# Block-sparse attention with a mixture of experts: the sparse scores of a tile's two query blocks in one stretch of TensorE's program

## The chip, the core and the metric

The kernel runs on one core of a Trainium2 chip. A core has engines that run side by side, each with an instruction queue of its own that it works off in order: TensorE (PE; PEld is its loading of weights), VectorE (DVE), ScalarE (ACT), GpSimd (POOL), and SyncE (SP), which issues most DMAs. Matmul results go to PSUM, which has eight banks of 128 partitions x 512 fp32 numbers. The engines wait for each other by semaphores. The metric is the device time of one execution in microseconds (us); lower is better.

## The reference

`q`, `k`, `v` are 4 batches x 8 heads x 768 tokens x 64. Tokens form 24 blocks of 32. A query block sees its own block and its two neighbours, the first and the last block, and three sampled blocks; the first and last query blocks see all keys. Each token's attention output (512 numbers over all heads) then goes to one of 8 experts.

```python
scores = scale * np.matmul(q, k.transpose(0, 1, 3, 2))
mask = np.abs(blk_i - blk_j) <= window
mask = mask | (blk_i == 0) | (blk_j == 0) | (blk_i == n_blocks - 1) | (blk_j == n_blocks - 1)
for qb in range(n_blocks):
    for kb in sampled_blocks[qb]:
        mask[qb * block:(qb + 1) * block, kb * block:(kb + 1) * block] = True
attn = np.exp(scores - max) / (sum + 1e-09)          # over the keys with mask
x = (attn @ v)                                       # 3072 tokens x 512
...
logits = x @ w_gate + modality_bias[modality_id]
e_idx = np.argmax(logits, axis=1)
out = gate_w * (np.maximum(x @ w1[e_idx], 0.0) @ w2[e_idx])
```

## The kernel before

**Two stages.** First attention for 24 tiles of 128 tokens (two of them are the "dense" blocks that see all keys), with the gate's logits and the ranking of tokens by expert beside it; then the experts, a matrix product in three fp32r parts per group of 256 tokens. The change is in the first stage.

**A sparse tile.** Batches come in halves of two (HB = 2). Per half there are NM = 11 sparse tiles; a tile is two neighbouring query blocks (n = 0 and 1) of both batches of the half, all 8 heads. That makes 22 tiles and, with n and the batch b, four items per tile, in the order (n, b) = (0,0), (0,1), (1,0), (1,1). A query block sees 8 key blocks. POOL copies the keys into `kbuf` (lines 466 to 482): slots 0 to 7 are the eight for n = 0 and slots 4 to 11 those for n = 1, so four are shared.

**Steps of an item** (letters as in the code) and their lines:
- S, `scores` (line 533): 16 matmuls, 64 rows x 32 columns of the array each, fp32, for both batches of one n, so it is done once per n, at the item with b = 0. It writes two fresh banks. An fp32 matmul is two passes, so a block of scores shows as 32 records.
- M, `masked` (541, DVE): adds the mask and takes the maximum; it reads and, with the last item, frees the scores' banks.
- X, `exps` (549, ACT); T, `transposed` (558, PE: four 128x128 transposes into a bank); A, `copied` (563, ACT: out of that bank).
- per tile: W, `weigh_shared` (580, PE) and V, `sum_rows` and `weigh_own` (573, 589, PE), O, `divide` (440 to 442, DVE: frees V's and W's banks), Y, `turned` (596 PE, 598 ACT), G, the gate (606 PE, 609 DVE), then small DVE work for the routing (295 to 368).

Dense items have the same letters: scores 379, maxima 392 to 395, exp 401 and 402, transposes 411, copies 418, weighing 431 and 433.

**What sets the order.** Each engine's program in this stage is written in the order of the code. A loop over ticks t does, for every step, the item k = t - LAG[step]; LAG says how many ticks behind its scores an item's step stands (M 1, X 2, T and A 4, W 5, V 7, O 8, Y 10, G 13 for sparse items). Within a tick the steps come in the order of ORDER. Items of the second half's dense blocks are put between sparse items 21|22, 29|30, 45|46 and 47|48 (DENSE_AFTER). Items 21, 29 and 45 have (n, b) = (0, 1), so in the sixth, eighth and twelfth tile two dense items stand between the n = 0 and the n = 1 items. The opening of the program, the first tile and part of the second, is a list written by hand (START).

**PSUM.** All eight banks come from one pool; `bank()` hands out a free one, and the first write into it waits until its last reader is done. A block of scores takes two banks, a transpose, a weighing, a gate one each; a pair of dense scores takes four.

Of the kernel before, what the change touches and what calls it, by code (L numbers as in the profile page):

```python
# [38 lines left out]
HB = 2  # L39
NM = NB // 2 - 1  # L40
# [49 lines left out]
def attention_moe(ctx, tc, kD, qD, qH, v0, v1, blocks, modality, w_gate, bias, w1, w2, out):  # L90
# [29 lines left out]
    with ExitStack() as actx:  # L120
# [5 lines left out]
        def bank():  # L126
            return psum.tile([P, 512], F32, name="bank")
# [244 lines left out]
        def dense_scores(b, pr):  # L372
            q = qd[b // HB]
            s1, s2 = zip(*[(bank(), bank()[:, 0:256]) for _ in range(2)])
            for o, blocks_ in ((s1, slice(0, 16)), (s2, slice(16, 24))):
                for c in range(2):
                    for u in range(2):
                        r, col = slice(64 * u, 64 * u + 64), 64 * (u ^ c)
                        nc.tensor.matmul(o[c][col:col + 64, :], lhsT=q[r, b % HB * NPAIR + pr + c], rhs=kd[b][r, pr // 2, blocks_, c * 32:c * 32 + 32],
                                         start=True, stop=True, tile_position=(64 * u, col))  # L380
            return zip(s1, s2)
# [8 lines left out]
        def dense_max(b, pr, s1, s2):  # L390
            nm2 = small.tile([P, 2], F32, name="nm2")
            nc.vector.tensor_reduce(nm2[:, 0:1], s1, axis=AX.X, op=ALU.max, negate=True)
            nc.vector.tensor_reduce(nm2[:, 1:2], s2, axis=AX.X, op=ALU.max, negate=True)
            nb_ = small.tile([P, 1], F32, name="nb_")
            nc.vector.tensor_scalar(nb_, nm2[:, 0:1], nm2[:, 1:2], 0.125, ALU.min, ALU.mult)
            return s1, s2, nb_

        def dense_exp(b, pr, s1, s2, nb_):
            a = work.tile([P, 768], F32, name="a", bufs=5)
            sm = small.tile([P, 2], F32, name="sm", bufs=6)  # L400
            nc.scalar.activation(a[:, 0:512], s1, AF.Exp, bias=nb_, scale=0.125, accum_out=sm[:, 0:1])  # L401
            nc.scalar.activation(a[:, 512:768], s2, AF.Exp, bias=nb_, scale=0.125, accum_out=sm[:, 1:2])
            return a, sm

        def dense_transpose(b, pr, a, sm):
            tps = []
            for k0, k1 in ((0, 4), (4, 6)):
                tp = bank()
                tps.append((k0, k1, tp))
                for k in range(k0, k1):  # L410
                    nc.tensor.transpose(tp[:, (k - k0) * P:(k - k0 + 1) * P], a[:, k * P:(k + 1) * P], ident)
            return tps, sm

        def dense_copy(b, pr, tps, sm):
            at = ad[0]
            ad.append(ad.pop(0))
            for k0, k1, tp in tps:
                (nc.vector.tensor_copy if (b, pr) in DENSE_DVE else nc.scalar.copy)(at[:, k0:k1, :].rearrange("p a b -> p (a b)"), tp[:, 0:(k1 - k0) * P])
            su = small.tile([P, 1], F32, name="su", bufs=4)
            nc.vector.tensor_tensor(su, sm[:, 0:1], sm[:, 1:2], ALU.add)  # L420
            return at, su


        def dense_weigh(b, pr, at, su):
            o = bank()
            for k in range(-1, 6):
                for u in range(2):
                    h, col = 2 * pr + u, 64 * (u ^ pr % 2)
                    r = slice(64 * u, 64 * u + 64)
                    if k < 0:  # L430
                        nc.tensor.matmul(o[r, D:D + 1], lhsT=ident[:, col:col + 64], rhs=su, start=True, stop=False, tile_position=(0, 64 * u))
                    else:
                        nc.tensor.matmul(o[r, 0:D], lhsT=at[:, k, col:col + 64], rhs=vd[b][:, k, D * h:D * h + D],
                                         start=False, stop=k == 5, tile_position=(0, 64 * u))
            return (o,)
# [89 lines left out]
        def scores(q, g, n):  # L525
            s0 = 4 * n
            kv = kbuf[g % 2].rearrange("p s (b r f) -> p s b r f", b=HB, r=NPAIR)
            sp = [bank(), bank()]
            for b in range(HB):
                for pr in range(NPAIR):  # L530
                    for u in range(2):
                        r = slice(64 * u, 64 * u + 64)
                        nc.tensor.matmul(sp[u][32 * pr:32 * pr + 32, b * 256:(b + 1) * 256], lhsT=q[r, b * NPAIR + pr, n, :],  # L533
                                         rhs=kv[r, s0:s0 + 8, b, pr, :], start=True, stop=True, tile_position=(64 * u, 32 * pr))
            return sp
# [682 lines left out]
        qraw, o_s = {}, {}  # L1218
# [39 lines left out]
        for g in range(2 * NM):  # L1258
            half, m = divmod(g, NM)
# [20 lines left out]
        st, done = {}, set()  # L1280

        def do(op, it):
            if (op, it) in done:
                return
            done.add((op, it))
            if it[0] == "d":
                _, b, pr = it
                half = b // HB
                if op == "S":
                    if pr % 2 == 0:  # L1290
                        for c, o in enumerate(dense_scores(b, pr)):
                            st["d", b, pr + c] = o
                elif op == "M":
                    st[it] = dense_max(b, pr, *st[it])
                elif op == "X":
                    st[it] = dense_exp(b, pr, *st[it])
                elif op == "T":
                    st[it] = dense_transpose(b, pr, *st[it])
                elif op == "A":
                    st[it] = dense_copy(b, pr, *st[it])  # L1300
                elif op == "W":
                    st[it] = dense_weigh(b, pr, *st[it])
                elif op == "O":
                    if (b % HB, pr) == (0, 0):
                        new_tile(-1, half)
                    dense_out(b, pr, *st.pop(it))
                elif (b % HB, pr) == (HB - 1, NPAIR - 1):
                    if op == "Y":
                        turns[-1, half] = turned(xrs[-1, half])
                    elif op == "G":  # L1310
                        end_tile(-1, half)
            else:
                _, half, m, n, b = it
                if op == "S":
                    if b == 0:
                        sp = scores(qraw[m, half], half * NM + m, n)
                        for b_ in range(HB):
                            st["s", half, m, n, b_] = sp
                elif op == "M":
                    st[it] = masked(m, n, b, st[it])  # L1320
                elif op == "X":
                    if (n, b) == (0, 0):
                        sums[m, half] = small.tile([P, 4, 2], F32, name="sums", bufs=4)
                    st[it] = exps(sums[m, half][:, 2 * b + n, :], *st[it])
                elif op == "T":
                    st[it] = transposed(n, st[it])
                elif op == "A":
                    if n == 0:
                        ats[m, half, b] = work.tile([P, 16, 2, 32], F32, name="at", bufs=NAT)
                    copied(n, b, st.pop(it), ats[m, half, b])  # L1330
                    if (n, b) == (1, HB - 1):
                        sums[m, half] = spread(sums[m, half])
                elif (n, b) == (1, HB - 1):
                    if op == "W":
                        st[it] = bank()
                        weigh_shared(half * NM + m, st[it], [ats[m, half, b_] for b_ in range(HB)])
                    elif op == "V":
                        banks[m, half] = bank()
                        sum_rows(sums.pop((m, half)), banks[m, half])
                        weigh_own(half * NM + m, st[it], [ats[m, half, b_] for b_ in range(HB)])  # L1340
                    elif op == "O":
                        new_tile(m, half)
                        divide(st.pop(it), banks.pop((m, half))[:, 0:H], slice(0, P), H, xrs[m, half][:, 0:HD])
                    elif op == "Y":
                        turns[m, half] = turned(xrs[m, half])
                    elif op == "G":
                        end_tile(m, half)
# [98 lines left out]
```

## Time and profile before

| | us |
|---|---|
| median of 3 runs | 539.94 |
| the runs | 538.39, 539.94, 546.9 |
| the profiled execution | 535.39 |
| its span, first to last instruction | 533.7 |
| score matmuls (line 533), first and last start | 23.5, 215.1 |

All times in the rows below are from that one profiled execution, in us from the span's start. A timeline row has the start, the length (from the first start to the last end of the instructions that the row merges), engine, line, operation, the tile written <- the tiles read, the shape, the count, and in brackets how long the engine had been idle before and what ended that. PE's instructions overlap: the next one starts long before the row's end. A row of a group has the busy time in total, the mean length of one instruction in ns, and the idle time before its instructions.

### The profile page before, as it was taken

The page shows a single profiled execution, that of the slowest core. Times are in us where ns is not written, and L with a number is a line of the kernel's source. Part 1 is how long each engine was busy: PE and PEld are TensorE (multiplying, and loading weights), DVE is VectorE, ACT ScalarE, POOL GpSimd, SP SyncE. Part 2 cuts the span into 40 slices and gives each one's busy share as a digit, 9 for nine tenths or more (in the row PEclk, how much of TensorE's full clock was granted, in tenths as well). Part 3 has the DMA queues.
Part 4 walks back from the last instruction along what each step waited for, and adds up shares of the span by engine and source line. Part 5 has one row for each costly group of instructions (what it writes and reads, how often), then busy time and mean ns, then how long its engine had stood idle before and what let it go on. Part 6 is the DMA issues. An engine that isn't in the chain of part 4 may idle for free.

```text
span 533.7 us, 19015 instructions
## 1 busy us (share of the span) xinstructions
PE 512.8 (96%) x7298; PEld 433.4 (81%) x7298; DVE 378.7 (71%) x1139; ACT 335.4 (63%) x765; POOL 214.7 (40%) x451
## 2 busy tenths in 40 slices
PE   8999999998999999899999999999999999999995
PEld 6667676776778777788989898998989899898984
DVE  7995588677778999967996655556565555656553
ACT  3689877977888977935456454646545464554552
POOL 3578675666458886123155123030312303031213
PEclk9999999999999999999999999999999999999999
DMA  7985886999646888965788776676757667675740
GB/s 281 339 243 150 234 252 209 249 223 242 205 144 205 209 217 233 277 206 206 237 280 305 237 253 201 239 252 204 239 191 244 211 222 250 206 243 192 249 150 23
DMA packets 49443, 119.44 MB, mean 224 GB/s; under 512 B 7744, under 2 KB 8128, under 8 KB 49344
## 3 DMA queue, kind: packets, MB, share of 16 engines
q1 hardware_dynamic: 45248, 105.02, 64.6%
q0 software_dynamic: 4096, 13.12, 6.9%
q8 instruction: 59, 0.97, 0.8%
q14 instruction: 40, 0.33, 0.2%
HBM read 105.52 MB, written 12.86 MB: 222 GB/s over the span
## 4 chain that ended last, share of the span: by engine, by line
issue 41%; PE 32%; DVE 11%; DMA 7%; POOL 5%; SPq 3%; ACT 1%; POOLq 0%; DVEq 0%; ACTq 0%
PE bank L533 5%; PE bank L558 5%; DMA out<-slot,si 3%; PE bank L589 3%; DVE y L541 3%; POOL slot L736 3%; DMA slot<-v 3%; PE bank L580 2%; POOL out L790 2%; PE bank L606 2%; PE bank L754 1%; PE bank L770 1%; PE bank L771 1%; PE bank L769 1%; PE bank L755 1%
## 5 line engine op out<-in xcount | busy, mean ns | idle before, releaser
L725 DVE TENSOR_TENSOR slot<-slot 128x1024 fp32r<-128x1024 f32 x99 | 122.8, 1245 | 89.5 <-ACT slot L722 87.7
L722 ACT CAST slot<-slot 128x1024 fp32r<-128x1024 f32 x104 | 108.1, 1048 | 104.1 <-PE bank L755 50.1
L754 PE MATMUL bank<-slot 128*128 128x256 f32 x384 | 108.4, 282 | 0.0
L756 PE MATMUL bank<-slot 128*128 128x256 f32 x384 | 107.7, 281 | 0.0
L755 PE MATMUL bank<-slot 128*128 128x256 f32 x384 | 107.6, 280 | 0.0
L790 POOL DMA_INDIRECT out<-slot,si x20 | 25.4, 1270 | 178.6 <-ACT slot L786 175.6
L549 ACT ACTIVATE a<-y,mn 128x256 f32<-128x256 f32 x176 | 88.6, 511 | 10.3 <-DVE mn L541 10.2
L769 PE MATMUL bank<-slot 128*128 128x512 f32 x192 | 76.6, 399 | 0.0
L770 PE MATMUL bank<-slot 128*128 128x512 f32 x192 | 75.9, 395 | 0.0
L771 PE MATMUL bank<-slot 128*128 128x512 f32 x192 | 75.7, 394 | 0.0
L754 PEld LDWEIGHTS bank<-slot 128*128 128x128 f32 x384 | 72.2, 188 | 0.6
L755 PEld LDWEIGHTS bank<-slot 128*128 128x128 f32 x384 | 72.1, 188 | 0.4
L756 PEld LDWEIGHTS bank<-slot 128*128 128x128 f32 x384 | 72.2, 188 | 0.0
L541 DVE CUSTOM_DVE_ANT_1 y<-bank,smask 128x256 f32<-128x256 f32 x176 | 66.3, 417 | 0.4
L482 POOL COPY slot<-slot 128x128 f32 x264 | 63.9, 295 | 0.0
L563 ACT COPY at<-bank 128x512 f32<-128x512 f32 x88 | 50.7, 577 | 9.9 <-PE bank L558 9.9
L504 POOL TENSOR_SCALAR slot<-slot 32x1024 f32<-32x1024 f32 x40 | 41.6, 1041 | 35.4 <-issue 11.6
L558 PE MATMUL bank<-ident,a 128*128 128x128 f32 x352 | 51.9, 280 | 0.8 <-ACT a L401 0.5
L533 PE MATMUL bank<-slot,q_raw 64*32 64x256 f32 x1408 | 49.4, 382 | 1.5 <-issue 0.6
L771 PEld LDWEIGHTS bank<-slot 128*128 128x128 f32 x192 | 36.1, 188 | 8.4
L770 PEld LDWEIGHTS bank<-slot 128*128 128x128 f32 x192 | 36.1, 188 | 7.8 <-DVE slot L725 0.4
L558 PEld LDWEIGHTS bank<-ident,a 128*128 128x128 f32 x352 | 38.1, 140 | 4.9 <-ACT a L549 0.8
(302 smaller groups left out, 852.9 us busy)
## 6 DMA issues: line engine op xcount, KB each, us to landing
slot<-w SPq DMA_DIRECT2D x100, 512.0 KB, 4.1
slot<-v SPq DMA_DIRECT2D x180, 128.0 KB, 3.9
x_d<-xr SPq DMA_DIRECT2D x22, 256.5 KB, 5.0
q_raw<-qH SPq DMA_DIRECT2D x22, 256.0 KB, 4.8
slot<-v SPq DMA_DIRECT2D x16, 256.0 KB, 4.6
slot<-kD SPq DMA_DIRECT2D x13, 256.0 KB, 4.3
slot<-v SPq DMA_DIRECT2D x4, 768.0 KB, 11.8
slot<-w SPq DMA_DIRECT2D x10, 256.0 KB, 4.1
```

The costliest lines, as they stand in the source:

```text
L533: nc.tensor.matmul(sp[u][32 * pr:32 * pr + 32, b * 256:(b + 1) * 256], lhsT=q[r, b * NPAIR + pr, n, :], rhs=kv[r, s0:s0 + 8, b, pr, :], st ...
L541: nc.vector.tensor_tensor_reduce(y[:, u, :].rearrange("p (s f) -> p s f", s=8), sp[u][:, b * 256:(b + 1) * 256].rearrange("p (s f) -> p s ...
L549: nc.scalar.activation(a[:, u, :], y[:, u, :], AF.Exp, bias=mn[:, u:u + 1], scale=-1.0, accum_out=total[:, u:u + 1])
L558: nc.tensor.transpose(tp[:, k:k + P], a[:, u, c * P:(c + 1) * P], ident)
L722: nc.scalar.copy(h, s)
L725: (eng or (nc.gpsimd if n in POOL_SPLITS else nc.vector)).tensor_tensor(l, s, h.bitcast(F32), ALU.subtract)
L754: nc.tensor.matmul(o, lhsT=h[:, fs], rhs=xh[g % 2][:, c, :], start=c == 0 and f % 2 == 0, stop=False)
L755: nc.tensor.matmul(o, lhsT=h[:, fs], rhs=xl[g % 2][:, c, :], start=False, stop=False)
L756: nc.tensor.matmul(o, lhsT=l[:, fs], rhs=xh[g % 2][:, c, :], start=False, stop=c == 3 and f % 2 == 1)
L769: nc.tensor.matmul(o, lhsT=hh[0][:, f, ts_], rhs=h[:, fs], start=f == 0, stop=False)
L770: nc.tensor.matmul(o, lhsT=hh[0][:, f, ts_], rhs=l[:, fs], start=False, stop=False)
L771: nc.tensor.matmul(o, lhsT=hl[f // 4][:, f % 4, ts_], rhs=h[:, fs], start=False, stop=f == 7)
```

## The change

The n = 1 block of scores of a tile is computed where its n = 0 block is, directly behind it, in all tiles but the first of the first half (whose scores stand in the hand-written opening). The four banks are taken at that place; everything else of the code stays.

```diff
                 if op == "S":
                     if b == 0:
-                        sp = scores(qraw[m, half], half * NM + m, n)
-                        for b_ in range(HB):
-                            st["s", half, m, n, b_] = sp
+                        for n_ in (n,) if (half, m) == (0, 0) else range(2) if n == 0 else ():
+                            sp = scores(qraw[m, half], half * NM + m, n_)
+                            for b_ in range(HB):
+                                st["s", half, m, n_, b_] = sp
```

Only PE's program changes its order; the same instructions stand on DVE, ACT, POOL and SP in the same order. On PE the number of instructions is the same too. Three places follow. L533 are the scores, L558 a tile's transposes, L573 and L589 step V, L580 step W, L596 step Y, L606 the gate; `x16` is one block of scores.

PE, an ordinary tile (its second block is the first row with a minus, the next tile's blocks follow):

```order
 L596 MATMUL bank<-ident,xr 128x128 x4
 L558 MATMUL bank<-ident,a 128x128 x4
-L533 MATMUL bank<-slot,q_raw 32x256 x16
 L573 MATMUL bank<-rexp,fold 32x8 x4
 L589 MATMUL bank<-slot,at 32x64 x32
 L558 MATMUL bank<-ident,a 128x128 x8
-L533 MATMUL bank<-slot,q_raw 32x256 x16
+L533 MATMUL bank<-slot,q_raw 32x256 x32
 L606 MATMUL bank<-wg_raw,xT 64x8 x8
 L580 MATMUL bank<-slot,at 64x64 x16
```

The second block has left its place between transposes and step V, and stands ahead of the gate and step W, five rows earlier in its own tile.

PE, the eighth tile, which has dense scores (L379) between its two blocks and the dense step O (L431, L433) behind the first; the program before:

```order
L533 MATMUL bank<-slot,q_raw 32x256 x16
L431 MATMUL bank<-su,ident 64x1 x2
L433 MATMUL bank<-slot 64x64 x12
L580 MATMUL bank<-slot,at 64x64 x16
L558 MATMUL bank<-ident,a 128x128 x8
L379 MATMUL bank<-slot,qd 64x512 x4
L379 MATMUL bank<-slot,qd 64x256 x4
L606 MATMUL bank<-wg_raw,xT 64x8 x8
L573 MATMUL bank<-rexp,fold 32x8 x4
L589 MATMUL bank<-slot,at 32x64 x32
L558 MATMUL bank<-ident,a 128x128 x8
L533 MATMUL bank<-slot,q_raw 32x256 x16
```

and the changed one:

```order
L533 MATMUL bank<-slot,q_raw 32x256 x32
L431 MATMUL bank<-su,ident 64x1 x2
L433 MATMUL bank<-slot 64x64 x12
L580 MATMUL bank<-slot,at 64x64 x16
L558 MATMUL bank<-ident,a 128x128 x8
L379 MATMUL bank<-slot,qd 64x512 x4
L379 MATMUL bank<-slot,qd 64x256 x4
L606 MATMUL bank<-wg_raw,xT 64x8 x8
L573 MATMUL bank<-rexp,fold 32x8 x4
L589 MATMUL bank<-slot,at 32x64 x32
L558 MATMUL bank<-ident,a 128x128 x8
L580 MATMUL bank<-slot,at 64x64 x16
```

The second block moved ahead of ten rows, the dense scores among them; behind the last transposes step W now follows at once.

PE, the last tile, with the semaphores that an instruction waits for (a name is the engine whose progress is awaited):

```order
 L533 MATMUL bank<-slot,q_raw 32x256 [waits DVE_49]
 L533 MATMUL bank<-slot,q_raw 32x256 x14
-L606 MATMUL bank<-wg_raw,xT 64x8 [waits DVE_49]
+L533 MATMUL bank<-slot,q_raw 32x256 [waits DVE_49,Pool_49]
+L533 MATMUL bank<-slot,q_raw 32x256 [waits DVE_49]
+L533 MATMUL bank<-slot,q_raw 32x256 x6
+L533 MATMUL bank<-slot,q_raw 32x256 [waits Pool_49]
+L533 MATMUL bank<-slot,q_raw 32x256 x7
+L606 MATMUL bank<-wg_raw,xT 64x8 [waits Activation_49]
 L606 MATMUL bank<-wg_raw,xT 64x8 x7
```

The second block's first two matmuls, one for each of its banks, wait for DVE, which by the program's counts has to finish lines 440 and 442 of step O first; the gate now takes a bank that ACT has to free.

## The prediction

> **What bounds the kernel now.** I read the page first: the span, the engines' shares and the slices of time.
>
> ```profile
> span 533.7 us, 19015 instructions
> PE 512.8 (96%) x7298; PEld 433.4 (81%) x7298; DVE 378.7 (71%) x1139; ACT 335.4 (63%) x765; POOL 214.7 (40%) x451
> PE   8999999998999999899999999999999999999995
> DVE  7995588677778999967996655556565555656553
> PEclk9999999999999999999999999999999999999999
> ```
>
> TensorE (PE) is busy nearly throughout and its clock is never throttled. The score matmuls (line 533) run in the first 40% of the span, and there VectorE (DVE) has slices of 9 too. So I asked for the engines' busy time by stage.
>
> ```profile
> 44.00:60.00 16.00, 14.86 (x415) 11.49 (x417) 10.04 (x50) 14.09 (x48) 11.96 (x33) 1.00 0.78 211
> 82.00:95.00 13.00, 12.13 (x291) 8.93 (x289) 10.78 (x49) 9.37 (x31) 6.42 (x19) 1.00 0.66 204
> 193.00:201.00 8.00, 7.70 (x220) 6.01 (x219) 7.68 (x38) 6.12 (x21) 6.81 (x20) 1.00 0.87 229
> 201.00:209.00 8.00, 7.97 (x214) 6.18 (x212) 7.81 (x41) 7.43 (x24) 4.75 (x11) 1.00 0.82 238
> 300.00:360.00 60.00, 60.00 (x399) 54.78 (x398) 35.63 (x38) 29.85 (x37) 14.01 (x12) 1.00 0.71 232
> ```
>
> The columns are the length, then busy time of PE, its weight loads, DVE, ACT, POOL, then clock and DMA. The mixture of experts (300 to 360) has PE busy for all of 60.00: whatever the attention stage gains or loses arrives at the end undiminished. In the attention stage it is not one engine: from 193 to 209 DVE is busy 7.68 and 7.81 of 8.00, as much as PE. A tile is a loop PE, DVE, ACT, PE, and a saving on PE counts only where that loop has slack.
>
> **What the change saves: changes of the array's shape.** An ordinary tile, PE's timeline (start, length, what):
>
> ```profile
> 47.09 0.60 PE L596 MATMUL bank<-ident,xr 128*128 128x128 f32 x4
> 47.52 0.60 PE L558 MATMUL bank<-ident,a 128*128 128x128 f32 x4
> 48.05 1.09 PE L533 MATMUL bank<-slot,q_raw 64*32 64x256 f32 x32
> 49.08 0.25 PE L573 MATMUL bank<-rexp,fold 128*32 128x8 f32 x8
> ```
>
> Four transposes followed by more transposes take 47.52 - 47.09 = 0.43 us; four followed by the scores take 48.05 - 47.52 = 0.53. Going into the 64x32 shape costs 0.10. The scores hold PE for 49.08 - 48.05 = 1.03. The 32 passes last 1.09 from the first start to the last end.
>
> ```profile
> L533 PE MATMUL bank<-slot,q_raw 64*32 64x256 f32 x1408 | 49.4, 382 | 1.5 <-issue 0.6 <-DVE xrd L452 0.5 <-DMA q_raw<-qH 0.4
> ```
>
> One pass is 0.382 long, so the starts spread over 1.09 - 0.38 = 0.71 us. Eight tile positions run side by side, so that is four rounds with three intervals, at most 0.24 each, about 0.22. A second block of 16 matmuls in the same stretch thus costs 4 x 0.22 = 0.87 instead of 1.03: 0.16 saved. The way in (0.10) is saved as well only where the neighbours left behind have one shape; here they are 128*128 (L558) and 128*32 (L573), so a change stays. I take 0.16 per tile; 21 tiles make 3.4 us, the most I give the change on this account (0.26 in each would be 5.5).
>
> The Trainium skill, page TensorEngine Tiling (Array Packing), section Key Properties, says that a change of tiling mode drains the array. If a drain meant waiting for the whole matmul in flight, removing one would save about that flight, 0.38 per tile, and the sum would be 8.0 us, an estimate from the rule. The rows do not bear that out: the way in costs 0.10 while a pass lasts 0.38, so most of the flight is overlapped.
>
> Added work: none. No instruction, DMA or byte is added, and DVE, ACT, POOL and SP keep their order; only PE's moves. The second block now needs POOL's gathered keys 0.87 us after the first one's start, some us earlier than before. The tightest tile is the one at 36.48:
>
> ```profile
> 32.77 2.91 POOL L482 COPY slot<-slot 128x128 f32 x11
> 36.48 1.10 PE L533 MATMUL bank<-slot,q_raw 64*32 64x256 f32 x32 [0.46 <-DVE xrd L452]
> ```
>
> The copies end at 35.68, the second block is due at 36.48 + 0.87 = 37.35: hidden by 1.7 us, cost nothing. Queries are one load for both blocks, so SP has no new deadline.
>
> **What it costs: 0.87 us in front of everything behind the first block, and two more banks held.** In PE's queue the second block now stands ahead of the gate (L606), the weighing (L580), the transposes and, in three tiles, the dense scores (L379); all of these come 0.87 later, and who waits for them waits longer. Where it used to stand nothing covers ACT's copies any more. The tile where this bites, PE, then DVE, then ACT:
>
> ```profile
> 82.21 1.09 PE L533 MATMUL bank<-slot,q_raw 64*32 64x256 f32 x32
> 87.61 0.64 PE L606 MATMUL bank<-wg_raw,xT 128*64 128x8 f32 x16
> 89.27 1.10 PE L558 MATMUL bank<-ident,a 128*128 128x128 f32 x8
> 90.30 1.09 PE L533 MATMUL bank<-slot,q_raw 64*32 64x256 f32 x32
> 93.09 0.66 PE L558 MATMUL bank<-ident,a 128*128 128x128 f32 x4 [0.54 <-ACT a L401]
> 95.05 0.44 PE L411 MATMUL bank<-ident,a 128*128 128x128 f32 x2 [0.36 <-ACT a L401]
> ```
>
> ```profile
> 88.30 0.17 DVE L609 TENSOR_TENSOR lg<-bank,btok 128x8 f32<-128x8 f32 x1 [1.25 <-PE bank L606]
> 89.43 0.69 DVE L442 TENSOR_TENSOR xr<-bank,rt 128x512 f32<-128x512 f32 x1 [0.46 <-PE bank L589]
> ```
>
> ```profile
> 82.11 0.58 ACT L598 COPY xT<-bank 128x512 f32<-128x512 f32 x1
> 90.73 0.57 ACT L563 COPY at<-bank 128x512 f32<-128x512 f32 x1
> 92.26 0.69 ACT L401 ACTIVATE a<-bank,nb__2462 128x512 f32<-128x512 f32 x1 [0.96 <-DVE nb__2462 L395]
> ```
>
> Read as a loop: DVE waits 1.25 us for PE's gate and 0.46 for L589, ACT waits 0.96 for DVE, PE waits 0.54 and 0.36 for ACT. Every link is bound, so 0.87 at 82.21 becomes 0.87 at 93.09. The 1.03 given back at 90.30 is worth nothing: behind the transposes (ending 89.27 + 1.10 = 90.37) PE would come to L580 at once, and the bank it needs is let go by ACT's copy ending 90.73 + 0.57 = 91.30; the scores had covered that. To this comes the wait for the second block's own banks: the copy at 82.11 ends at 82.69, due is 82.21 + 0.87 = 83.08, a slack of 0.39, less than the 0.87 that the tile before may hand on: up to 0.48 more, and once more the 0.87 that is handed on. Lower end 0.87, upper end 0.87 + 0.48 + 0.87 = 2.2. I take 2.0, near the upper end, because this loop has no idle link to work a lag off.
>
> Two more tiles have dense scores between their blocks, so that two of the eight banks are held 7.6 and 9.7 us:
>
> ```profile
> 59.96 1.09 PE L533 MATMUL bank<-slot,q_raw 64*32 64x256 f32 x32
> 67.56 1.26 PE L533 MATMUL bank<-slot,q_raw 64*32 64x256 f32 x32
> 119.80 1.09 PE L533 MATMUL bank<-slot,q_raw 64*32 64x256 f32 x32
> 123.57 0.97 PE L580 MATMUL bank<-slot,at 128*64 128x64 f32 x25 [1.83 <-issue]
> 129.50 1.09 PE L533 MATMUL bank<-slot,q_raw 64*32 64x256 f32 x32
> ```
>
> I price the first at 0.9 (the lower end: the tiles before it run with PE ahead), the second at 1.5 (between the ends: its 1.83 of idle time with no releaser could swallow part). The three together: 4.4, bounds 2.6 and 6.6.
>
> The late tiles, from 185 on, run at DVE's pace. The last one:
>
> ```profile
> 209.03 1.09 PE L533 MATMUL bank<-slot,q_raw 64*32 64x256 f32 x32
> 210.46 0.64 PE L606 MATMUL bank<-wg_raw,xT 128*64 128x8 f32 x16 [0.33 <-DVE rt L440]
> 211.52 1.15 PE L580 MATMUL bank<-slot,at 128*64 128x64 f32 x32 [0.43 <-issue]
> 214.15 1.36 PE L533 MATMUL bank<-slot,q_raw 64*32 64x256 f32 x32
> ```
>
> ```profile
> 210.73 0.69 DVE L442 TENSOR_TENSOR xr<-bank,rt 128x512 f32<-128x512 f32 x1
> ```
>
> Its second block, due at 209.90, has to wait for the bank that DVE reads until 211.42. It then ends the stretch near 211.42 + 0.87 + 0.16 = 212.45, and the gate comes 2.0 later than at 210.46; the 0.43 behind it is absorbed and the 1.03 of the old place is given back: + 0.6. The other three late tiles lie between -0.16 (DVE keeps up) and + 0.87 (bound like the tile at 82); I take the middle, 0.35, since DVE is neither idle nor all of the limit: + 1.05. Late tiles: + 1.6, bounds 0.1 and 3.2.
>
> **The sum.** 21 tiles are merged: 3 with dense scores between, 4 late ones, 14 ordinary. 14 x (-0.16) = -2.2; dense + 4.4; late + 1.6: together + 3.8 us. The profiled execution took 535.39 with a span of 533.7, and would become 539.2; the median of the runs is 539.94, 4.55 above it, and the sum on that is 543.7.
>
> **The rivals.**
> The other side: banks are always free in time and the loop absorbs 0.87. Then each tile gains 0.16 and the time is 539.94 - 3.4 = 536.5. For it: PE's waits for banks are hardly seen before (1.5 us idle in all ahead of L533). Against it: the bound loop at 82 to 95. It decides at the slack of DVE's gate and ACT's copies: above 0.87 in all three dense tiles it wins. Its far end is that each change of shape costs the whole flight of a pass, 0.38: 21 x 0.38 = 8.0 and 532; the 0.10 of the way in speaks against that. [...]
> Nothing to measure: the gain of the ordinary tiles and the dense tiles' loss cancel because waits at L401 reset PE's lead either way: 540.
> The loop is bound in every tile: 21 x 0.87 = 18.3 us more, 558. For it: 7.81 of 8.00 on DVE late. Against it: from 44 to 60 DVE is busy 10.04 of 16.00 and can catch up.
>
> **How the numbers follow.** My forecast, between + 0.5 and + 9 us: chance 0.60. Gain on all tiles: 0.18, of which 0.03 for the drain in full. Cancelled: 0.13. Bound in every tile: 0.09. Range: low 536.5, the first rival; high 549.0, which takes the upper bounds of the dense and late tiles, 6.6 + 3.2, with half of the ordinary gain lost: 6.6 + 3.2 - 1.1 = 8.7 and rounding. About 2% is what a measurement of this kernel can tell from no change, that is 529 and 551. Slower by over 2%: 0.09 and little else, 0.09; faster by over 2%: 0.03; within 2%: 0.88.
>
> **What would show it.** Right: the line of the scores gathers fewer switches, 23 stretches on PE instead of 44, each pair 1.9 us long; the waits of PE L533, L580 and L606 for ACT L563 and for DVE grow by several us; DVE's wait for L606 grows; attention ends some 4 us later. If the last scores' tile ends earlier and DVE's wait for L606 has not grown, the loop had slack and I am wrong. If PE's lag grows evenly over all tiles, the third rival is right. If the lag is only at 60 to 72, 82 to 95 and 120 to 131, the banks held across the dense scores are the cause.

## The result, and the profile after

The changed kernel takes 542.87 us (median of 6 runs, 541.92 to 544.55). Against the runs of before beside them its ratio is 1.0141, interval 1.0103 to 1.0178, so about 7.6 us (5.5 to 9.6) slower. Run once more on another occasion it took 543.29 us with a ratio of 1.0100 (1.0057 to 1.0143), 5.4 us. Both lie within 2%. All ratios compare fast executions alone: the 546.9 among before's three runs is not in them, nor are four of the experiments' executions that took 656 to 1247 us. The forecast was 543.7, 3.8 us more than before. The profiled execution took 543.24 us with a span of 541.5, that of before 533.7.

The page of the changed kernel, span, engines and two rows of the slices:

```profile
span 541.5 us, 19001 instructions
PE 516.4 (95%) x7298; PEld 440.6 (81%) x7298; DVE 374.9 (69%) x1139; ACT 335.0 (62%) x765; POOL 216.2 (40%) x451
PE   8999898997999999889999999999999999999995
PEclk9999999998999999999999999999999999999999
```

PE's share falls from 96% to 95% with the same 7298 records. Of the 7.8 us by which the span grew, 4.2 are idle time of PE and 3.6 are busy time, although no work was added; part of that is a stretch at half the clock, the one 8 that is new in the clock's row, of which more below. Two groups of PE's line view:

```profile
L533 PE MATMUL bank<-slot,q_raw 64*32 64x256 f32 x1408 | 47.5, 380 | 4.5 <-issue 2.7 <-DMA q_raw<-qH 0.5 <-DVE rt L440 0.4
L580 PE MATMUL bank<-slot,at 128*64 128x64 f32 x704 | 26.7, 228 | 4.1 <-issue 3.2 <-POOL slot L504 0.9
```

The scores are busy for 47.5 us instead of 49.4: the shared stretches save something. POOL is not among the three largest releasers of the scores: its keys are in time, but for one place named below. The view of the waits, first of before, then of the changed kernel (us in total, times, the longest):

```profile
ACT at L563 <- PE bank L558: 9.9, 13, 1.7
DVE lg L609 <- PE bank L606: 7.5, 10, 1.3
```

```profile
ACT at L563 <- PE bank L558: 19.6, 17, 4.8
DVE lg L609 <- PE bank L606: 15.9, 15, 2.8
```

DVE waits twice as long for the gate, ACT twice as long for the transposes: PE brings later what the others need. The place, in PE's timeline of the changed kernel, is the first tile with dense scores between its blocks (it starts at 59.96 in before):

```profile
57.21 1.96 PE L533 MATMUL bank<-slot,q_raw 64*32 64x256 f32 x64
59.09 0.64 PE L606 MATMUL bank<-wg_raw,xT 128*64 128x8 f32 x16
...
65.25 0.25 PE L573 MATMUL bank<-rexp,fold 128*32 128x8 f32 x8 [0.30 <-ACT at L563]
...
67.49 0.66 PE L558 MATMUL bank<-ident,a 128*128 128x128 f32 x4 [0.23 <-DVE xr L442]
...
69.58 1.15 PE L580 MATMUL bank<-slot,at 128*64 128x64 f32 x32 [0.87 <-POOL slot L504]
```

The stretch with both blocks takes 59.09 - 57.21 = 1.88 us. Behind the dense scores PE then waits three times: 0.30 and 0.23 for banks, and 0.87 ahead of step W, where the second block used to stand.

Where the 7.8 us of the span come from, from the starts of the same instructions in both traces: the tile at 59.96 +2.8, that at 82.21 +2.1, that at 119.80 +4.2, together +9.1; all other attention about -1.5; the experts +0.3. So the cost sits in the three tiles that the prediction named. The experiments ask whether that is the change or chance, and what in those tiles it is.

### The profile page after: what moved, and what is told of

It is laid out like the page before. It is cut to its first block, busy times and chain, and to the rows that moved or that the text cites. A ratio compares the mean times of both kernels' runs of the same rounds, so it can differ in the third digit from the quotient of the medians.

```text
span 541.5 us, 19001 instructions
## 1 busy us (share of the span) xinstructions
PE 516.4 (95%) x7298; PEld 440.6 (81%) x7298; DVE 374.9 (69%) x1139; ACT 335.0 (62%) x765; POOL 216.2 (40%) x451
## 4 chain that ended last, share of the span: by engine, by line
issue 41%; PE 29%; DVE 9%; DMA 8%; POOL 6%; ACT 3%; SPq 2%; POOLq 1%; ACTq 0%; DVEq 0%
PE bank L533 7%; PE bank L558 6%; PE bank L589 4%; PE bank L580 3%; DMA slot<-v 3%; POOL slot L736 3%; DMA out<-slot,si 2%; POOL out L790 2%; PE bank L606 2%; DMA slot<-x_d,gi 2%; PE bank L596 1%; PE bank L433 1%; DVE slot L725 1%; PE bank L411 1%; SPq L521 1%
## 5 line engine op out<-in xcount | busy, mean ns | idle before, releaser
L504 POOL TENSOR_SCALAR slot<-slot 32x1024 f32<-32x1024 f32 x40 | 42.5, 1062 | 56.4 <-PE bank L589 31.4
L482 POOL COPY slot<-slot 128x128 f32 x264 | 63.9, 293 | 0.0
L563 ACT COPY at<-bank 128x512 f32<-128x512 f32 x88 | 50.7, 576 | 19.6 <-PE bank L558 19.6
L558 PE MATMUL bank<-ident,a 128*128 128x128 f32 x352 | 53.2, 282 | 1.3 <-DVE xr L442 0.7
L533 PE MATMUL bank<-slot,q_raw 64*32 64x256 f32 x1408 | 47.5, 380 | 4.5 <-issue 2.7
L558 PEld LDWEIGHTS bank<-ident,a 128*128 128x128 f32 x352 | 38.3, 141 | 6.2 <-DVE xr L442 1.4
```

Source lines behind the costliest of these rows:

```text
L558: nc.tensor.transpose(tp[:, k:k + P], a[:, u, c * P:(c + 1) * P], ident)
```

## The experiments

The tiles are counted from 0 here; 5, 7 and 11 are the three with dense scores between their blocks, "crossing" below. us are the ratio times 538, the median of before.

**Only the crossing tiles, and all but them.** In place of the diff's condition:

```diff
-for n_ in (n,) if (half, m) == (0, 0) else range(2) if n == 0 else ():
+for n_ in (n,) if half * NM + m not in (5, 7, 11) else range(2) if n == 0 else ():
```

> Only the sixth, eighth and twelfth tile are merged, the three that have dense scores between their two blocks; the other 18 tiles stand as before. Theory T (the cost sits in these three): the trace of the changed kernel is 2.8, 2.1 and 4.2 us later behind them, 9.1 in all, so +9 us on 537.3, ratio 1.017 (1.012 to 1.020). Rival E (each merged tile costs the same): 7.6 us over 21 tiles is 0.36 each, three make +1.1, ratio 1.002. Rival I (PE's idle time with no releaser, which in the changed kernel is 2.74 at 125.03 and 1.62 at 225.07 against 1.83 and 0.31 before, makes most of the difference): +2.2 only, if both fall in the same places, ratio 1.004.

Measured: 1.0112 (1.0044 to 1.0180), +6.0 us from three tiles. The other way round, merging all but those (condition `in (0, 5, 7, 11)`):

> The other 18 tiles are merged, the three with dense scores between their blocks stand as before. Theory T: the rest of the changed kernel's lag, 7.8 - 9.1 = -1.3 us, ratio 0.998 (0.995 to 1.000). Rival E: 18 x 0.36 = +6.5 us, ratio 1.012. Rival I: +2.2 or what stalls there are, ratio 1.004.

Measured: 1.0004 (0.9968 to 1.0041), +0.2 us from eighteen tiles. An even cost, rival E, is out on both sides. Theory T stands, with less than the 9 that one pair of traces gave and just under the 1.012 at which its range began. Rival I's 1.004 lies just below the first interval and inside the second, so these two times alone do not put it out; the rows without such idle times, further down, do.

**The others, early and late.** Merged alone: tiles 1 to 4, 6 and 8 to 10; then tiles 12 to 21.

> Only the early tiles without dense scores between their blocks are merged: the second to fifth, the seventh, and the ninth to eleventh, eight of 22. By the terms of the prediction 8 x (-0.16) = -1.3 us, ratio 0.998. By the trace of the changed kernel (2.75 us earlier by the sixth tile, 1.6 more over the seventh, nothing over the ninth to eleventh) up to -4 us, ratio 0.992. Rival E: 8 x 0.36 = +2.9, ratio 1.005.

> Only the last ten tiles of 22 are merged, behind the last dense scores. By the terms of the prediction: six ordinary ones -1.0, four late ones +1.6, together +0.6 us, ratio 1.001 (0.998 to 1.004). Rival (the late loop on DVE is bound in each): 10 x 0.87 = +8.7, ratio 1.016. The trace of the changed kernel is 2.9 us later over this stretch, of which 1.3 at one idle time of PE without a releaser: ratio 1.003 to 1.005 if that falls there again.

Measured: early 0.9969 (0.9934 to 1.0003), -1.7 us; late 1.0025 (0.9989 to 1.0062), +1.3 us. The late loop bound in each tile (1.016) is out. The two signs are as forecast, but each interval reaches to no change.

**The banks alone.** Before's order, with the first two of the second block's sixteen matmuls, one for each of its banks, moved ahead in the crossing tiles:

```diff
-            sp = [bank(), bank()]
+            sp = st.pop(("held", g), None) or [bank(), bank()]; nx = [bank(), bank()] if n == 0 and g in (5, 7, 11) else None
-            for b in range(HB):
-                for pr in range(NPAIR):
-                    for u in range(2):
+            for b, n_, bk in ((0, n, sp), (1, n, sp), *(((0, 1, nx),) if nx else ())):
+                for pr in range(NPAIR) if bk is not nx else (0,):
+                    for u in range(2) if n == 0 or (b, pr) != (0, 0) or not g in (5, 7, 11) else ():
...
+                                         rhs=kv[r, 4 * n_:4 * n_ + 8, b, pr, :], start=True, stop=True, tile_position=(64 * u, 32 * pr))
-            return sp
+            return st.update({("held", g): nx} if nx else {}) or sp
```

> Before's order, but in the three tiles with dense scores between the blocks the first two of the second block's sixteen matmuls, one for each of its two banks, stand behind the first block; the other fourteen stay where they were. So the banks are held as in the change, while only about an eighth of 0.87 us of PE's work is moved ahead. Theory Ta (the cost is the two of eight banks held across the dense scores): most of the 9 us remains, +6 to +9 us, ratio 1.011 to 1.017. Theory Tb (the cost is 0.87 us of work put in front of a loop PE, DVE, ACT, PE that is bound): three times an eighth, +0.3 us, ratio 1.001 and at most 1.003. Half and half would show as 1.006 to 1.009.

Measured: 1.0088 (1.0044 to 1.0131), +4.7 us, in the band named for half and half; Theory Tb alone (at most 1.003) is out, the lower part of Ta's range is not. PE's timeline, the first and the third crossing tile:

```profile
59.75 1.49 PE L533 MATMUL bank<-slot,q_raw 64*32 64x256 f32 x36
61.17 0.41 PE L606 MATMUL bank<-wg_raw,xT 128*64 128x8 f32 x8
...
66.00 0.25 PE L573 MATMUL bank<-rexp,fold 128*32 128x8 f32 x8 [0.30 <-ACT at L563]
...
68.16 0.66 PE L558 MATMUL bank<-ident,a 128*128 128x128 f32 x4 [0.23 <-DVE xr L442]
...
121.35 2.03 PE L533 MATMUL bank<-slot,q_raw 64*32 64x256 f32 x36
```

The two bank waits, 0.30 and 0.23, are those of the full change, to the hundredth: they come from holding two banks, since the run with the work alone, next, has neither. In the third tile the 36 records last 2.03, in the first 1.49: there the matmuls into the held banks wait as well. One thing was wrong in the expectation: the two moved matmuls are not an eighth of 0.87. The 36 records hold PE for 61.17 - 59.75 = 1.42 us where a block of 32 holds it for 1.02, and the 28 left behind still take 1.01. So 0.4 us per tile, 1.2 of the 4.7, are work in front of the loop; by itself that would be a ratio of 1.002, below the interval.

**The work alone.** Before's order and banks, the first block computed twice in the crossing tiles:

```diff
-            for b in range(HB):
+            for b in (0, 1, 0, 1) if n == 0 and g in (5, 7, 11) else range(HB):
```

> Before's order and banks; in the three tiles with dense scores between the blocks the first block is computed twice in its stretch, into the same banks, so that 0.87 us of work is put in front of the loop, no bank is held longer, and the second block keeps its place. This adds 3 x 0.87 = 2.6 us of work to PE. Theory Tb (the loop is bound and the cost of the change is what is put in front of it): +2.6 us or more, each tile as much later as the change makes it (2.8, 2.1, 4.2), ratio 1.005 to 1.017. Theory Ta (banks): the work alone is partly absorbed by PE's waits in these stretches, 0 to +2.6 us, ratio 1.000 to 1.005.

Measured: 1.0049 (1.0009 to 1.0090), +2.6 us, the number of Tb for the bare work, but also the most that Ta allowed, so this time alone does not choose between them. No bank waits now in any of the three tiles; the second:

```profile
81.41 1.96 PE L533 MATMUL bank<-slot,q_raw 64*32 64x256 f32 x64
...
88.23 0.25 PE L573 MATMUL bank<-rexp,fold 128*32 128x8 f32 x8
...
89.33 1.09 PE L558 MATMUL bank<-ident,a 128*128 128x128 f32 x8
```

So both theories hold a part. The intervals of the two runs overlap, so their order by size is not shown by the times. Without the 1.2 us of work in the first run, banks and work are 3.5 + 2.6 = 6.1 us, beside the 6.0 of the whole; each of these is known to some 2 us.

**Is the room left behind worth anything?** Crossing tiles merged, and the second block computed once more at its old place, into the same banks; to the condition of the first experiment:

```diff
-for n_ in (n,) if half * NM + m not in (5, 7, 11) else range(2) if n == 0 else ():
+for n_ in (n,) if half * NM + m not in (5, 7, 11) else (0, 1) if n == 0 else (1,):
```

> Only the three tiles with dense scores between the blocks are merged, as in the run of that kind before, and at its old place the second block is computed once more, into the same banks: 3 x 1.03 = 3.1 us of PE's work more than that run. Theory C (the room that the block leaves behind is worth nothing, because step W there waits 0.87, 0.56 and 0.87 us for a bank that ACT's copy frees): the extra blocks fill that idle time, 3.1 - 2.3 = +0.8 us against that run, so 1.010 to 1.014 of before, and the idle time ahead of L580 at these three places is gone. Rival (the room is used): +3.1 us against it, ratio 1.017.

Measured: 1.0103 (1.0054 to 1.0152), with 3.1 us more of PE's work no slower than the run without it (1.0112). Two intervals of this width leave 4 us either way, so the times do not put out the rival's 3.1; the rows have to. In its timeline the idle time ahead of step W is gone at all three places; the first:

```profile
68.92 1.09 PE L533 MATMUL bank<-slot,q_raw 64*32 64x256 f32 x32
69.94 0.64 PE L606 MATMUL bank<-wg_raw,xT 128*64 128x8 f32 x16
70.43 1.15 PE L580 MATMUL bank<-slot,at 128*64 128x64 f32 x32
```

From the first score to step W it takes 10.98 and 11.26 us in the first and second crossing tile; the run without the extra blocks took 11.98, of which 0.78 was a stop without releaser, and 10.86. An extra block of 1.02 us of work costs nothing in the one and 0.4 in the other: the room is worth next to nothing there. (At the third the two runs cannot be compared, since the clock was halved in this one.) One thing was wrong in that expectation: by the program's counts it is ACT's copy that W waits for in the second tile alone; in the first and third it is ACT's exponentials of dense scores (L401), which free one of the dense scores' banks. The changed kernel there, first DVE, then ACT:

```profile
65.56 0.17 DVE L440 TENSOR_SCALAR rt<-bank 128x8 f32<-128x8 f32 x1 [4.25 <-PE bank L573]
...
66.74 0.69 DVE L442 TENSOR_TENSOR xr<-bank,rt 128x512 f32<-128x512 f32 x1 [0.77 <-PE bank L589]
67.35 0.68 DVE L392 TENSOR_REDUCE nm<-bank 128x1 f32<-128x512 f32 x1
```

```profile
68.71 0.69 ACT L401 ACTIVATE a<-bank,nb__1864 128x512 f32<-128x512 f32 x1 [0.83 <-DVE nb__1864 L395]
69.29 0.19 ACT L401 ACTIVATION_READ_ACCUMULATOR a<-bank,nb__1864 128x1 f32 x1
```

It is a closed loop: DVE has idled 4.25 us for PE's step V and 0.77 more for its second part, only then comes to the dense maxima, ACT waits 0.83 for those and ends its exponential at 69.29 + 0.19 = 69.48, and PE's step W starts at 69.58. In the second profile the same gap of 0.1 us lies between L401's end and step W, and in the second tile of both it lies between L563's end and step W. (The row of W above names POOL's L504, which it awaits as well.) Whatever stands ahead of V on PE, the moved block and the bank wait of 0.30, moves the whole loop, and PE comes to W early for nothing.

**Dense scores moved out from between the blocks.** `DENSE_AFTER` set to (23, 31, 47, 51), so that no tile is crossing; first with before's order of scores, then with the full change.

> Before's order of scores, but the pairs of dense items of the second half stand behind items 23, 31, 47 and 51 instead of 21, 29, 45 and 47, so that no tile has dense scores between its two blocks. It is the kernel against which the next one is read. By itself: the same work, PE's total unchanged; a dense pair's maxima and exponentials now meet other items, so anything from -4 to +5 us, ratio 0.993 to 1.009.

> The full change (21 tiles merged) on the kernel with the dense pairs between tiles. Theory T (what costs is that dense scores stand between the two blocks): the cost is gone, against that kernel -2 to +1 us, ratio to it 0.996 to 1.002. Rival E (each merged tile costs the same): +7.6 us against it, ratio 1.014. Rival B (banks are short wherever dense scores are near, and the merged blocks of the tile before or behind meet them as well): +4 to +8 us against it.

Measured: 1.0154 (1.0109 to 1.0200) and 1.0159 (1.0123 to 1.0195) of before. Merging costs nothing on top of the shift: 1.0005 between the two, the intervals leaving some 3 us either way. Theory T again, and rivals E and B, which wanted 4 us or more, are out. The kernel is another one, 8.3 us slower, and may have slack that before has not; that is not separated. That the shift by itself costs these 8.3 us was missed (at most 5 was expected). Its trace is late mainly from 160 us on; which part of the shift does that was not followed.

**Versions, and the sum.** Only the tiles over which the first trace gained; then the parts together.

> Only the second to fifth and the seventh tile are merged, those over which the trace of the changed kernel gains (2.75 and 1.6 us). By the prediction's price of a change of shape 5 x (-0.16) = -0.8 us, ratio 0.9985. If the gains of the trace are the change's own, -4 us, ratio 0.992. If they are PE's idle times without a releaser falling elsewhere, they average out and the first holds.

> The second to twelfth tile are merged, the three with dense scores between the blocks among them; the last ten stand as before. If the parts add up: +6.0 for those three and -1.7 for the other eight (from the runs of each alone), +4.3 us, ratio 1.008. If the whole of the changed kernel's 1.014 is already in these eleven tiles, the parts work on each other: the tiles that gain a lead hand it to the next crossing tile, where it is lost.

> The changed kernel itself, on the same chip as the run beside it. Its ratio was 1.0141 from 6 runs. The parts alone add up to +6.0 - 1.7 + 1.3 = +5.6 us, 1.0104: near that, the parts add up; near 1.014, some 2 us come only with all of them together.

Measured: tiles 1 to 4 and 6 alone 0.9973 (0.9937 to 1.0009), -1.5 us; tiles 1 to 11 1.0085 (1.0047 to 1.0123), +4.6 us where 6.0 - 1.7 = 4.3 was the sum; all of them 1.0100 (1.0057 to 1.0143), +5.4 where the sum was 5.6. The parts add up, as far as intervals of 2 us can tell. The best merged version is about 1.5 us ahead of before, not more than its interval: no gain is shown. Of the 4.3 us that the first trace gained over these tiles, 2.0 were two stops without a releaser in the trace of before (0.86 and 1.11 us).

**How much of the +4.2 at the third tile was chance.** The changed kernel's rows there, then its busy time by stretch (PE, its loads, DVE, ACT, POOL, then the granted clock, DMA share, GB/s):

```profile
120.35 1.94 PE L533 MATMUL bank<-slot,q_raw 64*32 64x256 f32 x58
125.03 0.63 PE L533 MATMUL bank<-slot,q_raw 64*32 64x256 f32 x6 [2.74 <-issue]
...
126.17 1.96 PE L580 MATMUL bank<-slot,at 128*64 128x64 f32 x32
```

```profile
125.00:127.00 2.00, 1.97 (x38) 1.56 (x39) 0.63 (x3) 0.00 (x0) 2.00 (x10) 0.74 0.95 233
127.00:129.00 2.00, 2.00 (x27) 1.88 (x24) 1.75 (x9) 0.00 (x0) 1.92 (x6) 0.50 0.95 237
```

PE stops in the middle of the scores for 2.74 us, waiting for nothing that the profile shows, and then runs at half its clock: step W takes 1.96 where it takes 1.13 to 1.15 elsewhere. In the second profile of the same kernel there is no such stop at that place, and the rows of the three tiles show the bare cost; second and third tile:

```profile
80.96 2.24 PE L533 MATMUL bank<-slot,q_raw 64*32 64x256 f32 x64
...
88.73 0.25 PE L573 MATMUL bank<-rexp,fold 128*32 128x8 f32 x8 [0.27 <-DVE lg L609]
...
90.98 0.66 PE L558 MATMUL bank<-ident,a 128*128 128x128 f32 x4 [0.23 <-DVE xr L442]
...
92.19 1.15 PE L580 MATMUL bank<-slot,at 128*64 128x64 f32 x32 [0.55 <-issue]
```

```profile
122.80 2.83 PE L533 MATMUL bank<-slot,q_raw 64*32 64x256 f32 x64
...
130.39 0.25 PE L573 MATMUL bank<-rexp,fold 128*32 128x8 f32 x8 [0.30 <-ACT at L563]
...
132.56 0.66 PE L558 MATMUL bank<-ident,a 128*128 128x128 f32 x4 [0.21 <-DVE xr L442]
...
134.65 1.15 PE L580 MATMUL bank<-slot,at 128*64 128x64 f32 x32 [0.87 <-issue]
```

The stretches are 2.24 and 2.83 long instead of 1.96: 0.28 and 0.87 of waiting for the second block's own banks. This wait varies: from 0 to 0.41 and from 0.60 to 0.87 over the profiles with these tiles merged. From the tile's first score to the start of step W behind its dense scores, the same work in each row but the second (0.4 us more) and the third:

| us, first score to step W (idle: idle time without releaser in it) | tile 5 | tile 7 | tile 11 |
|---|---|---|---|
| before | 9.58 | 9.19 | 11.65, 1.83 idle |
| banks alone | 10.50 | 10.78 | 12.88, 1.18 idle |
| first block twice (one block more) | 10.97, 0.31 idle | 10.05 | 11.41, begun at half clock |
| changed, second profile | 11.51, 0.24 idle | 11.23 | 11.86 |

Without those idle times the changed kernel's three tiles are 1.7, 2.0 and 2.0 us longer than before, 5.8 together: the first profile's 9.1 held some 3 us that come and go from run to run. They are a stop of 1.06 us in the first tile, 2.74 instead of 1.83 in the third, and the half clock behind it. With 5.8 us left where no such stop is counted, rival I is out as well.

## Why the prediction was right

**Direction and size.** Forecast +3.8 us, measured +7.6 on the first occasion and +5.4 on the second: the forecast is under the first interval and within the second. That the predicted 543.7 meets the measured 542.87 and 543.29 so closely is partly luck of the base: it was set on the three runs shown, with a median of 539.94 that the 546.9 had raised, while 17 to 29 later runs of before gave 537.8 to 538.1. On 538 the forecast would have been 541.8.

**The shape saving, 0.16 a tile: right.** A pair takes 1.88 us and two single blocks 2 x 1.02 to 2 x 1.03, so 0.16 to 0.18 is saved. Eight ordinary tiles alone were -1.7 us where 8 x 0.16 = 1.3. A drain for the whole flight of 0.38 would give 3.0 there; the times leave room for both, the pair's length decides for 0.16. The Trainium skill (page TensorEngine Tiling (Array Packing), section Key Properties) says that a change of mode drains the array. If the saving is that drain, it costs here a little under half of one flight; no run separates it from other costs of a change.

**The crossing tiles, +4.4 with bounds 2.6 to 6.6: right in place and kind, small in size.** Measured +6.0 (2.4 to 9.7) from the runs, 5.8 from the rows. By tile the rows gave 1.7, 2.0 and 2.0 us where 0.9, 2.0 and 1.5 were forecast. The term that was mis-sized is the wait for banks: it was put at 1.1 in the second tile and 0.6 in the third, 1.7 together, and left out in the first ("the tiles before it run with PE ahead"). The rows showed it in every one: 0.30 + 0.23, then 0.27 + 0.23 + 0.28, then 0.30 + 0.21 + 0.87, together 2.7 us. The prediction had only the wait of the second block for its own banks and a lag handed on by the tile before; the half microsecond that step V and the transposes behind it wait in every tile, because two of the eight banks are held, was not in it. That the second tile came out at the forecast 2.0 is therefore partly luck: its bank waits were 0.8, not 1.1. PE's lead does not help, since the wait is for ACT and DVE to empty the other six banks. The moved work itself, 3 x 0.87, was sized right (2.6 measured), and so, nearly, was its room being worth nothing. What frees step W's bank was named rightly for one tile of three.

**The third tile's 1.83 of idle time, said to "swallow part" of the cost: wrong.** It swallowed nothing: it was 2.74 in the first profile of the changed kernel and absent from that place in the second, which still lost 2.0 there. It is no slack; the last section shows what it is.

**The late tiles, +1.6: not refuted.** With six ordinary ones ahead (-1.0) the sum was +0.6; measured +1.3 (-0.6 to 3.3). The mechanism of the last tile, which the prediction worked out, came as forecast: the second block waits there for lines 440 and 442 on DVE, each of which frees one of its banks. The changed kernel:

```profile
215.27 1.09 PE L533 MATMUL bank<-slot,q_raw 64*32 64x256 f32 x32
216.71 0.59 PE L533 MATMUL bank<-slot,q_raw 64*32 64x256 f32 x2 [0.35 <-DVE rt L440]
217.64 1.09 PE L533 MATMUL bank<-slot,q_raw 64*32 64x256 f32 x30 [0.34 <-DVE xr L442]
218.66 0.52 PE L606 MATMUL bank<-wg_raw,xT 128*64 128x8 f32 x12
```

The gate follows 218.66 - 215.27 = 3.39 us behind the first score; the forecast was 212.45 - 209.03 = 3.42. Two tiles taken as ordinary, at 142.69 and 160.26, hold PE for 2.74 and 2.56 instead of 1.88, for waits that the sum did not have; the time of the late run shows no such cost at the end.

**POOL's keys at no cost: right but for one place.** In the tile at 160.26 the second block starts at 161.46, 0.03 us after one of POOL's copies (L482) has ended, and its weight loads had stood idle for 0.34 us before. The place watched, the tile at 36.48, was not the tightest.

**The rivals.** Gain only (536.5) and bound in every tile (558) are both out, the latter by eighteen merged tiles costing 0.2 us; that gain and loss cancel (no change) is outside both intervals of the changed kernel. Of the signs listed, the 1.9 us pairs, DVE's longer wait for the gate and the lag in just the three stretches came. By the prediction's own last sign that lag alone would have meant the held banks; the runs put about half of it on them and the rest on the moved work. Attention ended 7.6 later instead of 4 in that profile. The idle time of PE ahead of L580 did not grow in total (4.2 to 4.1): its waits moved to other places, and L573 and L558 were the ones to look at.

## What to carry to other kernels

In this kernel, grouping instructions to save changes of an engine's shape was worth 0.16 us a change where nothing long stood between the old place and the new, too little to show in the time. Across a step that itself takes half of PSUM, two more banks held cost 2.7 us of waits in three tiles, and the work moved ahead cost its full length because the room it left only became idle time. Before costing a removed block as gained time, look what the next instruction waits for: if it is freed by another engine at a fixed moment, the gain is nil or nearly so, and extra work put there costs little: a block of 1.02 us cost 0 and 0.4 us here. One pair of traces can carry 3 us of stalls that are no part of the change; merging parts alone and adding the ratios told them apart.

## What the runs showed of the hardware

**PE stops at fixed places of its program, and goes on when a packet of its instructions has landed.** Counting the matmul records in order, a stop without a releaser falls at record 2611 to 2614 in seven profiles, that of before, that of the changed kernel and those of five experiments, and another at 5009 to 5012 in five, though the kernels do different things at that count. At the first place they are 1.01 to 3.74 us long. The pages list a DMA queue of kind instruction, in before and in the changed kernel with 59 packets of 16 KB:

```profile
q8 instruction: 59, 0.97, 0.8%
```

The traces hold the time of every packet. In all seven the stop at 2611 to 2614 lies behind the 20th of them, and PE goes on 1.3 to 1.7 us after it has landed (in the changed kernel it lands at 123.47, and PE goes on at 125.03); in all five the stop at 5009 to 5012 lies behind the 39th, with 1.3 to 1.6 us. Of all stops without a releaser of 0.9 us or more, in fourteen profiles, each but one ends 1.2 to 2.0 us after a packet has landed. So PE waits there for its own instructions, as far as times can show it. The 20th packet sets out when PE is at record 2536 to 2614 in every profile, so the stop goes with PE's program and does not stand at a fixed time: a lag of PE cannot be worked off in it. Why the packet comes too late in one execution and not in another stays open.

**The clock is halved for 3.41 us at a time, and not by the length of a stop.** The run with the second block computed once more, after a stop of 3.74:

```profile
122.81 1.03 PE L558 MATMUL bank<-ident,a 128*128 128x128 f32 x8 [3.74 <-issue]
123.78 3.38 PE L533 MATMUL bank<-slot,q_raw 64*32 64x256 f32 x64
```

```profile
125.00:127.00 2.00, 2.00 (x43) 0.79 (x24) 0.00 (x0) 1.49 (x6) 2.00 (x9) 0.50 0.79 245
```

The same 64 records take 3.38 instead of 1.96, at a granted clock of 0.50. The stop of 2.74 in the changed kernel did the same; one of 2.78, in its second profile, did not:

```profile
105.71 0.56 PE L433 MATMUL bank<-slot 128*64 128x64 f32 x11 [2.78 <-issue]
```

What differs is how the stop lies on a grid. In every profile the half-clock stretches, but for the one at the span's end, last 3.41 us, in one case twice that, and each begins a whole multiple of 3.41 us after the clock was first granted in full. The stretches of that grid, first around the stop of 2.74, then around that of 2.78:

```profile
122.56:125.97 3.41, 0.94 (x20) 0.53 (x19) 1.06 (x5) 1.63 (x6) 3.24 (x12) 1.00 1.00 281
125.97:129.38 3.41, 3.41 (x48) 3.29 (x45) 2.38 (x11) 0.17 (x1) 3.33 (x13) 0.50 0.95 234
```

```profile
100.99:104.40 3.41, 1.94 (x35) 1.67 (x32) 2.24 (x11) 3.41 (x12) 3.33 (x10) 1.00 1.06 204
104.40:107.82 3.42, 2.11 (x55) 1.65 (x62) 1.39 (x7) 1.44 (x6) 1.57 (x7) 1.00 0.81 255
```

The first stop lies mostly in one stretch, with PE busy for 0.94 of 3.41 us, and the next stretch runs at 0.50. The second lies across a border, PE is busy for 1.94 and 2.11, and the clock stays at 1.00. Cut up so, the fourteen profiles have 23 full-clock stretches with PE busy for 42% or less, 14 of them at the span's end, and each is followed by half clock; of 2144 with 49% or more, five are, and what made those five was not followed.

The Trainium skill, page TensorE: Matmul & The Clock Gate, section Part 1: The HAM clock gate, says that the array falls to half its rate after at least one idle window of about 3.4 us. The two states and the length of the window agree with these rows; the window need not be wholly idle, since PE busy for up to 42% of it was little enough here.
